# Retention attention and a low-rank mixer on one core: the first loads in another order, unscaled queries, V spread by TensorE, zero matmuls in idle time

## The chip, the core and the metric

The kernel runs on one core of a Trainium2 chip, as one launch. A core has five engines with an instruction queue each, and each works through its queue in order: TensorE (PE, matmuls into PSUM), VectorE (DVE), ScalarE (ACT), GpSimd (POOL) and SyncE (SP), which issues most of the transfers between main memory and SBUF. GpSimd issues the stores. The metric is the time of the execution on the device in microseconds, the median of several runs, lower being better. The profile is of one execution, and its span runs from the first to the last instruction.

## What is computed

```python
# q, k, v: [8, 8, 576, 64] float32 (batch, heads, positions, head dim)
scores = scale * np.matmul(q, k.transpose(0, 1, 3, 2))        # scale = 1/8
gamma = 1.0 - 2.0 ** (-5.0 - np.arange(H))
rel = pos[:, None] - pos[None, :]
Dmat = np.where(rel >= 0, gamma[:, None, None] ** rel[None, :, :], 0.0)
attn = np.matmul(scores * Dmat[None], v)
x = attn.transpose(0, 2, 1, 3).reshape(B, S, H * D)           # [8, 576, 512]
h = x.transpose(0, 2, 1) @ U @ V                              # mixes positions, rank 32
u = x + h.transpose(0, 2, 1)
out = u + np.maximum(u @ w_ch1, 0.0) @ w_ch2                  # 512 -> 2048 -> 512
```

There is no softmax: the decay is gamma to the power of the distance, so a factor per position can be put on q (gamma to the position) and its inverse on k or v, and past positions can be carried on as a 64x64 state per head.

## The kernel before

**Tiles.** Positions are cut into chunks of 128 rows. A batch has 576 = 4 x 128 + 64 rows, so two batches make nine chunks: 0 to 3 of the even batch, 5 to 8 of the odd one, and chunk 4 (`XC`), whose halves belong to one batch each. The code calls a pair of batches `p`; for the first pair the halves of chunk 4 are loaded and worked on apart (`b=0`, `b=1`; XA and XB in the load order). Four chunks in a row, of either batch, are a group of 512 rows for the two layers of the mixer: nine groups in all (`mlp`, `g`).

**One chunk.** `load` (L388) brings k, q and v and casts them to bf16; v is multiplied by `vscale` (the inverse decay, L434). For the first pair q does not come chunk by chunk: `load_q4` (L330) loads 512 rows at once, four neighbouring rows to a partition, and L347 multiplies each quarter by `qs4`, the decay of its rows. `t_q4` (L355) and `t_pe` (L476) transpose q and k on TensorE; later pairs use transposing transfers (L469). `SC` (L550) makes the scores, and L583 multiplies them by the triangle `tri`. `ST` (L510) adds k-transposed times v to the running state in `ps_s`, copied out at L543; the last copy before chunk 4 goes to `sx` (L539) by two ScalarE instructions, one for each half of the partitions. `RV` (L614) makes scores times v plus q times state, evicted to `x_t`: for later pairs at L648 on VectorE, which applies `qscale`, and for the first pair at L660 or L662 as a plain copy, mostly on ScalarE.

**The mixer.** `MA` (L677) multiplies x by U into a 32-row block per chunk, evicted to `a_sb` (L701). V (32x576) must stand four times below itself in `VV` to meet these four blocks: `load_uv` (L857) loads it, casts it (L882), copies it down three times (L874) and once more, shifted, for the odd batch (L884), all on GpSimd. `build` (L749) makes the transposed u of the first two groups directly, and `MH` (L707) the untransposed one. `mlp` (L791) runs the hidden layer `Y1` (16 units of four matmuls of 128x512), whose eviction is L813, and the second layer `Y2` (16 units of four). The weights (16 transfers of 512 KB, `load_w` L887) are cast on GpSimd (L904, L922); six staging buffers take them, four of which lie in the second `y_t`.

**Order.** Nothing is ordered by hand within an engine: `Plan` takes every operation with its engine, an estimated duration, its dependencies, a priority and the buffers that it takes and gives back, simulates the five engines and one transfer ring, and issues the instructions of each engine in the order of its planned starts. On the chip each engine keeps this order and waits by semaphores, so an operation whose data come later than planned holds up all behind it. For transfers `DMA` (L324) has two figures, the time to issue and the time in the ring. The first pair's loads are in a fixed order, the list `line` at L1022: q of batch 0, k0, V, k1 to k3, k and q of XA, v0 to v3, v of XA, U, the weights, and then q of batch 1 and the odd batch's chunks.

A variable `filler` names a bank for matmuls in idle time, but no such matmul is issued. `zer` is set to zero and not used.

Of the kernel before, what the change touches and what calls it, by code (L numbers as in the profile page):

```python
# [28 lines left out]
class Plan:  # L29
# [11 lines left out]

    def pool(self, name, n, ordered=False):
        self.pools[name] = [0.0] * n
        if ordered:
            self.line[name] = []
# [7 lines left out]
    def run(self, hint=None):  # L53
        size = {name: len(x) for name, x in self.pools.items()}
        self.pools = {name: [0.0] * n for name, n in size.items()}
        self.held = {}
# [39 lines left out]
        def earliest(o):  # L96
            t = o.ready
            for pool, key in o.acq:
                if pool in self.line and self.line[pool][0] is not o:
                    return INF  # L100
                t = max(t, min(self.pools[pool]))
            return t

        wary = bool(hint)
        while left:
# [45 lines left out]
            for pool, key in o.acq:  # L151
# [5 lines left out]
                self.held[pool, key] = i  # L157
            for x in o.rel:
                self.n_rel[x] -= 1
                self.last[x] = max(self.last.get(x, 0.0), o.vis)  # L160
                if not self.n_rel[x]:
                    self.pools[x[0]][self.held[x]] = self.last[x]
            order.append((o, e))
# [10 lines left out]
def kernel(  # L174
# [42 lines left out]
    qs4 = sbuf("qs4", [P, 2, 4, H], FP32)  # L217
# [45 lines left out]
    def consts_a():  # L263
# [15 lines left out]
        for par in range(2):  # L279
            nc.gpsimd.iota(  # L280
                qs4[:, par, :, :], pattern=[[1, 4], [0, H]], base=par * P, channel_multiplier=4,
                allow_small_or_imprecise_dtypes=True,
            )
        for h in range(H):
            nc.vector.memset(lngt[:, :, h], lng[h])
        nc.vector.tensor_tensor(
            out=qs4.rearrange("p a r h -> p (a r) h"), in0=qs4.rearrange("p a r h -> p (a r) h"),
            in1=lngt[:, 0:8, :], op=ALU.mult,
        )
        nc.scalar.activation(out=qs4, in_=qs4, func=AF.Exp, bias=0.0, scale=1.0)  # L290
# [18 lines left out]
    filler = [ps_s]  # L309
# [20 lines left out]
    def load_q4(par, prio):  # L330
# [10 lines left out]
        got = ld["q4", par] = DMA(600.0, 3300.0, fn, prio=prio, acq=keys)  # L341
        for r in range(4):
            c = 5 * par + r

            def cast(e, r=r, c=c):
                eng = nc.gpsimd if e == "POOL" else nc.vector
                eng.tensor_tensor(  # L347
                    out=qkv[slot("qkv", (0, c))][:, 0, :, :], in0=q4v(r),
                    in1=qs4[:, par, r, :, None].to_broadcast([P, H, D]), op=ALU.mult)
            st["q", c] = pl.op("DVE", 700.0, cast, [got, ld["consts"]], prio + 0.1, acq=[("qkv", (0, c))],  # L350
                               rel=[keys[r]])
            if r == 3 and par == 0:
                st["q", c].engs = [("POOL", 1300.0)]
# [34 lines left out]
    def load(p, c, prio, early=False, b=None):  # L388
# [16 lines left out]
        for n, (j, dram) in enumerate(((1, k), (0, q), (2, v))):  # L405
# [10 lines left out]
            got[j] = DMA(480.0 if len(pts) == 1 else 900.0, 1220.0 if b is None else 620.0, fn,  # L416
# [28 lines left out]
        if early:  # L445
# [9 lines left out]
            elif c == XC:  # L455
                cv.engs.append(("DVE", 700.0))
        else:
# [52 lines left out]
    def ST(p, c, prio):  # L510
# [6 lines left out]
        def fn(e):  # L517
            if first:
                filler[0] = None
# [16 lines left out]
        def ev(e):  # L536
# [8 lines left out]
            )  # L545
        st["s", c] = st["s_ev"] = pl.op("ACT", 760.0 if c == XC - 1 else 600.0, ev, [o], prio, acq=[sk],
# [3 lines left out]
    def SC(p, c, prio, with_q=True, apart=False, b=None):  # L550
# [4 lines left out]
        rk = ("ret", (p, c))  # L555
        scks = [("big", ("sc", p, c, hl)) for hl in range(2)] if apart else [("sc", (p, kb))]
# [18 lines left out]
        o = pl.op("PE", (420.0 if n == P else 250.0) + (115 if with_q else 0), fn,  # L575
# [38 lines left out]
    def RV(p, c, prio, q_done=True, b=None, in_sc=False):  # L614
# [25 lines left out]
        if has_q:  # L640
            rel.append(("sx" if c == XC else "s_sb", (p, c - 1)))
        o = pl.op("PE", 230.0 + (130 if late else 0), fn,
                  [st["ret", kb], st["v", kb], st["s", c - 1] if late else None,
# [12 lines left out]
        def part(e, hls):  # L656
            args = dict(out=xs[slot(*xk)][rows].rearrange("p hp hl d -> p hl hp d")[:, hls],
                        in_=po[rows, hls, 0:NHP * D].rearrange("p hl (hp d) -> p hl hp d", d=D))
            if e == "ACT":
                i = nc.scalar.activation(func=AF.Copy, **args)  # L660
            else:
                i = nc.vector.tensor_copy(**args)  # L662
            st.setdefault(("xi", kb), []).append(i)
            if len(st["xi", kb]) == 2:
# [411 lines left out]
```

## Time and profile before

| | |
|---|---|
| median of 6 runs | 343.15 us (338.97 to 344.69) |
| the profiled execution | 342.83 us, span 340.6 us |
| mean granted TensorE clock | 0.999 |
| last v half of batch 0 scaled (VectorE) | 19.70 to 20.52 us |
| U products evicted (`a_sb`, ScalarE) | 25.64 to 26.24 us |
| first hidden matmul (`Y1` of group 0) | 27.60 us |
| q of batch 1 there, first cast | 49.47 us |
| first hidden matmul of group 1 | 72.43 us |

Times inside the profile count from the start of the span. Instructions that follow one another are merged in a timeline: a row has the start, the length of the stretch from the first start to the last end, and the count. A matmul's recorded length contains the time in the array; matmuls in a row start closer together (64 of 128x512 in 14.2 us). "[0.64 <-DMA st_st<-in_v_dram]" means that the engine was idle for 0.64 us before it, ended by that transfer.

### The profile page before, as it was taken

To read this page: it belongs to the slowest core of one execution; us is meant where nothing else is said; L and a number is where in the kernel's file an instruction comes from. 1 tells how busy PE (TensorE), PEld (TensorE's weight loads), DVE (VectorE), ACT (ScalarE), POOL (GpSimd) and SP (SyncE) were. 2 spreads that over 40 slices of the span, in tenths; PEclk is the share of its full clock that TensorE was granted. 3 is DMA by queue.
4 is the path that set the end of the run, shared out by engine and by line. 5 is a ranking of instruction groups with operands and counts; after the bars stand their busy time and mean duration, and the time that the engine had idled before them with its cause. 6 is when DMAs were issued, how large, how long until landed. Compare 5 with 4: busy or idle time off the path is not lost.

```text
span 340.6 us, 5977 instructions
## 1 busy us (share of the span) xinstructions
PE 322.1 (95%) x2420; PEld 159.6 (47%) x2420; DVE 144.7 (42%) x230; ACT 134.4 (39%) x239; POOL 87.4 (26%) x118
## 2 busy tenths in 40 slices
PE   0799979999999999999999999999999999999994
PEld 0564435556545544544455345544544444444442
DVE  3734028776655546555466356631543010020011
ACT  3466606468601660165214621354125306404600
POOL 5957636432231312132212112310110010010010
PEclk9999999999999999999999999999999999999999
DMA  8999999998999999999999999942110240011011
GB/s 206 200 272 391 381 209 219 240 231 169 220 212 186 250 188 215 172 242 201 197 194 257 158 200 220 246 94 42 68 64 15 49 107 31 0 64 62 0 59 66
DMA packets 153386, 56.18 MB, mean 165 GB/s; under 512 B 144752, under 2 KB 146800, under 8 KB 153360
## 3 DMA queue, kind: packets, MB, share of 16 engines
q1 hardware_dynamic: 150640, 46.90, 71.3%
q0 software_dynamic: 2720, 8.92, 7.6%
q8 instruction: 19, 0.31, 0.4%
q14 instruction: 7, 0.06, 0.1%
HBM read 36.92 MB, written 9.44 MB: 136 GB/s over the span
## 4 chain that ended last, share of the span: by engine, by line
PE 83%; DMA 6%; SPq 3%; DVE 3%; POOL 1%; issue 1%; ACT 1%; DVEq 0%
PE ps_big_t L302 68%; PE ps_s L302 5%; PE ps_o L302 5%; PE ps_sc L302 4%; DMA st_st<-in_k_dram 3%; SPq L412 3%; DMA vst<-in_moe_V_dram 2%; PE ps_big_t L492 1%; DMA q_st<-in_q_dram 1%; SPq L469 1%; DVE qkv_t L347 1%; DVE ret_t L583 1%; POOL VV L874 0%; DVE o_sb L837 0%; DVE u_t L730 0%
## 5 line engine op out<-in xcount | busy, mean ns | idle before, releaser
L302 PE MATMUL ps_big_t<-uT_t,w_sb 128*128 128x512 bf16 x576 | 133.5, 379 | 0.0
L302 PE MATMUL ps_big_t<-w_sb,y_t 128*128 128x512 bf16 x576 | 133.2, 379 | 0.0
L813 ACT ACTIVATE y_t<-ps_big_t 128x512 bf16<-128x512 f32 x144 | 86.0, 597 | 94.5 <-PE ps_big_t L302 93.8
L302 PEld LDWEIGHTS <-w_sb 128*128 128x128 bf16 x576 | 53.9, 98 | 61.7 <-issue 1.4
L302 PEld LDWEIGHTS <-y_t 128*128 128x128 bf16 x576 | 53.7, 98 | 60.9 <-issue 0.5
L837 DVE TENSOR_TENSOR o_sb<-ps_big_t,u_t 128x512 f32<-128x512 f32 x36 | 24.9, 690 | 99.8 <-PE ps_big_t L302 97.2
L843 POOL DMA_DIRECT2D out_dram<-o_sb x34 | 19.4, 570 | 153.6 <-DVE o_sb L837 153.6
L434 POOL TENSOR_TENSOR qkv_t<-st_st,vscale 128x512 bf16<-128x512 f32 x34 | 35.9, 1057 | 74.0 <-DMA st_st<-in_v_dram 60.8
L583 DVE TENSOR_TENSOR ret_t<-ps_sc,tri 128x1024 bf16<-128x1024 f32 x30 | 36.6, 1221 | 22.1 <-PE ps_sc L302 22.1
L543 ACT ACTIVATE s_sb<-ps_s 128x512 bf16<-128x512 f32 x28 | 16.7, 597 | 61.6 <-PE ps_s L302 61.5
L648 DVE TENSOR_TENSOR x_t<-ps_o,qscale 128x512 bf16<-128x512 f32 x27 | 18.6, 689 | 15.9 <-PE ps_o L302 15.9
L730 DVE TENSOR_TENSOR u_t<-ps_s,x_t 128x512 bf16<-128x512 f32 x20 | 13.8, 689 | 19.0 <-PE ps_s L302 18.9
L302 PEld LDWEIGHTS <-qkT_t 64*128 64x128 bf16 (+2 forms) x576 | 15.4, 100 | 12.0 <-issue 8.9
L302 PEld LDWEIGHTS <-ret_t 128*128 128x128 bf16 (+1 forms) x320 | 13.7, 103 | 8.0 <-DVE ret_t L583 1.6
L430 DVE CAST qkv_t<-st_st 128x512 bf16<-128x512 f32 x27 | 12.0, 445 | 9.3 <-DMA st_st<-in_k_dram 9.3
L302 PE MATMUL ps_o<-qkv_t,ret_t 128*128 128x64 bf16 (+1 forms) x304 | 14.6, 196 | 0.5 <-DVE ret_t L583 0.5
L430 DVE CAST qkv_t<-q_st 128x512 bf16<-128x512 f32 x27 | 12.1, 449 | 6.5 <-DMA q_st<-in_q_dram 6.4
L501 ACT ACTIVATE qkT_t<-ps_big_t 128x512 bf16<-128x512 bf16 (+1 forms) x21 | 11.4, 558 | 6.6 <-PE ps_big_t L492 6.5
L302 PE MATMUL ps_sc<-qkT_t 64*128 64x128 bf16 (+1 forms) x296 | 13.6, 219 | 0.3 <-DVE ret_t L583 0.3
L367 PE MATMUL ps_sc<-ident,qkv_t 128*128 128x128 bf16 x32 | 3.8, 264 | 10.6 <-DVE qkv_t L347 10.5
L302 PE MATMUL ps_s<-qkv_t 128*128 128x128 bf16 (+1 forms) x128 | 13.2, 229 | 0.3 <-ACT s_sb L543 0.3
L302 PEld LDWEIGHTS <-qkv_t 128*128 128x128 bf16 (+1 forms) x128 | 9.0, 101 | 6.0 <-issue 1.7
(81 smaller groups left out, 156.5 us busy)
## 6 DMA issues: line engine op xcount, KB each, us to landing
out_dram<-o_sb POOLq DMA_DIRECT2D x34, 256.0 KB, 3.8
st_st<-in_k_dram SPq DMA_DIRECT2D x32, 256.0 KB, 5.0
st_st<-in_v_dram SPq DMA_DIRECT2D x32, 256.0 KB, 5.4
q_st<-in_q_dram SPq DMA_DIRECT2D x24, 256.0 KB, 5.0
y_t<-in_moe_w_ch_dram SPq DMA_DIRECT2D x10, 512.0 KB, 8.0
wst_t<-in_moe_w_ch_dram SPq DMA_DIRECT2D x6, 512.0 KB, 8.0
q_st<-in_q_dram SPq DMA_DIRECT2D x2, 1024.0 KB, 8.6
st_st<-in_k_dram SPq DMA_DIRECT2D x8, 128.0 KB, 5.2
```

The lines of the kernel that those rows point to most:

```text
L302: nc.tensor.matmul(*a, skip_group_check=True, **kw)
L412: sent.append(nc.sync.dma_start(out=f[rw, :, :], in_=dram[bb, :, t0:t0 + rw.stop - rw.start, :].rearrange("h s d -> s h d"),))
L430: nc.vector.tensor_copy(**args)
L434: eng.tensor_tensor(out=qkv[slot(*qk)][rows, 2, :, :], in0=at(2)[rows], in1=vscale[rows, c, :, None].to_broadcast([rows.stop - rows.start, ...
L501: nc.scalar.activation(func=AF.Copy, **args)
L543: nc.scalar.activation(out=s_sb[slot(*sk)], in_=ps_s.rearrange("p (a b) -> p a b", b=P), func=AF.Copy)
L583: nc.vector.tensor_tensor(out=ret[slot(*rk)][rows, hl, :, 0:n], in0=bank(hl.start)[rows, None, :, 0:n] if apart else ps_sc[rows, hl, :, 0: ...
L648: nc.vector.tensor_tensor(out=xs[slot(*xk)][rows].rearrange("p hp hl d -> p hl hp d"), in0=po[rows, :, 0:NHP * D].rearrange("p hl (hp d) - ...
L730: nc.vector.tensor_tensor(out=us[slot(*uk)].rearrange("p (hp hl d) -> p hp hl d", hl=2, d=D), in0=bank().rearrange("p (hp hl d) -> p hp hl ...
L813: nc.scalar.activation(out=y1s[slot(*yk)][:, f, :], in_=ps_big[slot(*bk)], func=AF.Relu)
L837: nc.vector.tensor_tensor(out=osb[slot(*ok)], in0=ps_big[slot(*bk)], in1=us[slot(*uk)], op=ALU.add)
L843: eng.dma_start(out=out_flat[row:row + P, :], in_=osb[slot(*ok)])
```

## The change

- The fixed load order of the first pair is new. V moves behind U; the chunks of k and v take turns.
- q of the first pair is cast without a factor, on VectorE or ScalarE; the factor is put on at the x eviction, which so becomes the VectorE product for all whole chunks. `qs4` goes away. The halves of chunk 4 keep their scaled q and have a plain copy on ScalarE.
- V is cast by ScalarE and spread to 128 partitions by a matmul with `rep4`, four identities side by side, in two pieces by way of `ps_s`.
- The copy to `sx` before chunk 4, in the first pair, is one half on ScalarE and one on VectorE.
- Banks: the scores of chunk 4 go to `ps_sc`, and the product of chunk 1 to `ps_o`.
- The planner asks for as many free buffers as an operation takes of a pool; some estimates change; it keeps when buffers are held. Before the first `Y1`, where it sees TensorE idle for long enough and finds a bank free, zero matmuls of 128x512 are issued, up to 14 in one gap.

```diff
+    def idle(self, banks, a, b):
+        for x in banks:
+            if all(end < a or begin > b for begin, end in self.spans.get(x, [])):
+                return x
+        return None
...
-                t = max(t, min(self.pools[pool]))
+                n = sum(x[0] == pool for x in o.acq)
+                t = max(t, sorted(self.pools[pool])[n - 1])
...
-        for par in range(2):
-            nc.gpsimd.iota(
-                qs4[:, par, :, :], pattern=[[1, 4], [0, H]], base=par * P, channel_multiplier=4,
-                allow_small_or_imprecise_dtypes=True,
-            )
...
-        nc.scalar.activation(out=qs4, in_=qs4, func=AF.Exp, bias=0.0, scale=1.0)
+        for i in range(4):
+            nc.vector.tensor_copy(out=rep4[:, i * R:(i + 1) * R], in_=ident[0:R, 0:R])
...
-        got = ld["q4", par] = DMA(600.0, 3300.0, fn, prio=prio, acq=keys)
+        got = ld["q4", par] = DMA(600.0, 3900.0 - 600.0 * par, fn, prio=prio, acq=keys)
...
-                eng = nc.gpsimd if e == "POOL" else nc.vector
-                eng.tensor_tensor(
-                    out=qkv[slot("qkv", (0, c))][:, 0, :, :], in0=q4v(r),
-                    in1=qs4[:, par, r, :, None].to_broadcast([P, H, D]), op=ALU.mult)
-            st["q", c] = pl.op("DVE", 700.0, cast, [got, ld["consts"]], prio + 0.1, acq=[("qkv", (0, c))],
-                               rel=[keys[r]])
-            if r == 3 and par == 0:
-                st["q", c].engs = [("POOL", 1300.0)]
+                args = dict(out=qkv[slot("qkv", (0, c))][:, 0, :, :], in_=q4v(r))
+                if e == "ACT":
+                    nc.scalar.activation(func=AF.Copy, **args)
+                else:
+                    nc.vector.tensor_copy(**args)
+            st["q", c] = pl.op("DVE", 390.0, cast, [got], prio + 0.1, acq=[("qkv", (0, c))], rel=[keys[r]],
+                               alt=[("ACT", 640.0)])
...
-            got[j] = DMA(480.0 if len(pts) == 1 else 900.0, 1220.0 if b is None else 620.0, fn,
+            got[j] = DMA(480.0 if len(pts) == 1 else 900.0, 1220.0 if b is None else 900.0, fn,
...
+            elif c in (2, 3):
+                cv.engs.append(("DVE", 800.0))
...
+        if p == 0 and c == XC - 1:
+            insts = []
...
+            h = [pl.op(e, 390.0, lambda e, w=w: half(e, w), [o], prio, acq=[sk] if e == "ACT" else [],
+                       rel=[st["pss"]]) for e, w in (("ACT", slice(0, HALF)), ("DVE", slice(HALF, P)))]
...
-        if p:
+        def ev_x(e):
+            nc.scalar.activation(out=xs[slot(*xk)][rows].rearrange("p hp hl d -> p hl hp d"),
+                                 in_=po[rows, :, 0:NHP * D].rearrange("p hl (hp d) -> p hl hp d", d=D),
+                                 func=AF.Copy)
+        if b is None:
             st["x", kb] = [pl.op("DVE", 700.0, ev, [o], prio, rel=[pk])]
-        elif b == 0 or c == NCH - 1:
-            st["x", kb] = [pl.op(e, 400.0, lambda e, i=i: part(e, slice(i, i + 1)), [o], prio, rel=[pk])
-                           for i, e in enumerate(("ACT", "DVE"))]
         else:
-            st["x", kb] = [pl.op("ACT", 610.0, lambda e: part(e, slice(0, 2)), [o], prio, rel=[pk])]
+            st["x", kb] = [pl.op("ACT", 610.0, ev_x, [o], prio, rel=[pk])]
...
-        cv = pl.op("POOL", 600.0, lambda e: gp.tensor_copy(out=VV[0:R, 0:S], in_=vst), [ld["lv"]], -970.0)
-        ld["V"] = pl.op("POOL", 1500.0, rep, [cv], -970.0)
+        cv = pl.op("ACT", 640.0, lambda e: nc.scalar.activation(out=VV[0:R, 0:S], in_=vst, func=AF.Copy),
+                   [ld["lv"]], -935.0)
+        got = None
+        for i, (n, w) in enumerate((("V", slice(0, 4 * P)), ("Vx", slice(4 * P, S)))):
+            bk = ("pss", n)
+            m = w.stop - w.start
...
+                mm(ps_s[:, 0:m], rep4, VV[0:R, w], start=True, stop=True)
...
+                nc.scalar.activation(out=VV[:, w], in_=ps_s[:, 0:m], func=AF.Copy)
+            r = pl.op("PE", 230.0, fr, [cv, ld["consts"], got], -934.0 + 700.0 * i, acq=[bk])
+            got = ld[n] = pl.op("ACT", 600.0 - 300.0 * i, er, [r], -934.0 + 700.0 * i, rel=[bk])
...
-            SC(0, c, pr + 3, with_q=False, apart=c in (0, 2, XC), b=b)
+            SC(0, c, pr + 3, with_q=False, apart=c in (0, 2), b=b)
...
-            RV(0, c, pr + 1, q_done=False, b=0 if c == XC else None, in_sc=c in (1, 3))
+            RV(0, c, pr + 1, q_done=False, b=0 if c == XC else None, in_sc=c == 3)
...
-    line = [ld["q4", 0], ld["k", (0, 0)], ld["lv"]] + [ld["k", (0, c)] for c in range(1, 4)]
-    line += [ld["k", (0, XA)], ld["q", (0, XA)]]
-    line += [ld["v", (0, c)] for c in range(4)] + [ld["v", (0, XA)], ld["lu"]] + ld["lw"]
-    line += [ld["q4", 1]] + [ld[x, (0, XB)] for x in "kqv"]
-    line += [ld["k", (0, c)] for c in range(5, NCH)] + [ld["lub"]]
-    line += [ld["v", (0, c)] for c in range(5, NCH)]
+    line = [ld["q4", 0]] + L("k0 k1 v0 k2 v1 k3 v2 kA qA v3 vA") + [ld["lu"], ld["lv"]] + ld["lw"]
+    line += [ld["q4", 1]] + L("k5 kB k6 qB v5 vB k7 v6 k8") + [ld["lub"]] + L("v7 v8")
...
+    until = min(o.start for o in pl.ops if o.name == "Y1")
+    homes = {("big", i): ps_big[i] for i in range(3)}
+    homes["pss", 0] = ps_s
     with tc.manual_schedule():
+        at = 1000.0
         for o, e in order:
+            if e == "PE":
+                a, b = at + 60.0, o.start - 120.0
+                n = int((b - a) / 220.0)
+                if o.start <= until and n > 0:
+                    x = pl.idle(homes, a, b)
+                    if x is not None:
+                        for _ in range(min(n, 14)):
+                            mm(homes[x], zer[:, 0:P], zer, start=True, stop=True)
+                at = o.end
             o.fn(e)
```

## The prediction

> **What bounds the kernel now.** I read the page first (busy shares, the slices, the chain that ended last), then TensorE's waits, then busy time by stretch, then the timelines of TensorE, VectorE and GpSimd up to 75 us.
>
> ```profile
> PE 322.1 (95%) x2420; PEld 159.6 (47%) x2420; DVE 144.7 (42%) x230; ACT 134.4 (39%) x239; POOL 87.4 (26%) x118
> ...
> PEclk9999999999999999999999999999999999999999
> DMA  8999999998999999999999999942110240011011
> ...
> PE 83%; DMA 6%; SPq 3%; DVE 3%; POOL 1%; issue 1%; ACT 1%; DVEq 0%
> ```
>
> TensorE is busy 95% of the span and is 83% of the chain. The DMA row is full up to slice 26 (about 222 us), so an earlier TensorE can run into a late transfer. The waits of TensorE name where it stands still:
>
> ```profile
> PE ps_sc L367 <- DVE qkv_t L347: 10.5, 4, 7.3
> PE ps_big_t L302 <- ACT a_sb L701: 0.7, 1, 0.7
> ```
>
> Of the 10.5 us, 7.3 are the start and 2.1 lie at 48 to 50 us. By stretch (columns: TensorE, weight loads, VectorE, ScalarE, GpSimd, clock, DMA share, GB/s):
>
> ```profile
> 27.60:41.80 14.20, 14.20 (x67) 6.46 (x66) 3.11 (x6) 9.32 (x16) 9.93 (x10) 1.00 1.05 388
> 41.80:48.10 6.30, 6.28 (x30) 2.65 (x27) 0.69 (x1) 0.61 (x2) 3.83 (x4) 1.00 1.09 227
> 48.10:50.20 2.10, 0.00 (x0) 0.00 (x0) 0.73 (x2) 0.00 (x0) 0.01 (x1) 1.00 0.89 245
> 50.20:72.40 22.20, 21.75 (x256) 12.45 (x257) 16.62 (x24) 13.07 (x26) 10.90 (x13) 1.00 0.97 226
> ```
>
> The first hidden matmul starts at 27.60. From there to TensorE's last matmul at 336.4 there are 308.8 us, 305.1 of them busy in the same view: only 3.7 us of waiting is left. So the change can win in two places: an earlier 27.60, and less of those 3.7 us (2.13 at 48.1, 0.26 at 52.6, 0.49 at 150, 0.59 at 195). The lines of the timelines:
>
> ```profile
> 17.43 0.64 PE L302 MATMUL ps_o<-qkv_t,ret_t 128*128 128x64 bf16 x8
> ...
> 21.52 0.61 PE L302 MATMUL ps_big_t<-x_t,UU 128*32 128x512 bf16 x1
> 22.06 0.52 PE L302 MATMUL ps_s<-qkv_t 128*128 128x128 bf16 x4
> 22.42 0.40 PE L302 MATMUL ps_sc<-qkv_t,ret_t 128*128 128x64 bf16 x8
> ...
> 27.60 3.65 PE L302 MATMUL ps_big_t<-uT_t,w_sb 128*128 128x512 bf16 x16
> ```
>
> ```profile
> 19.70 0.82 DVE L434 TENSOR_TENSOR qkv_t<-st_st,vscale 64x512 bf16<-64x512 f32 x1 [0.64 <-DMA st_st<-in_v_dram]
> ...
> 66.71 0.98 DVE L430 CAST qkv_t<-q_st 128x512 bf16<-128x512 f32 x1
> ```
>
> ```profile
> 20.95 0.32 POOL L878 CAST UU<-ust 128x160 bf16<-128x160 f32 x1 [0.97 <-DMA ust<-in_moe_U_dram]
> 22.08 1.04 POOL L904 CAST w_sb<-wst_t 128x1024 bf16<-128x1024 f32 x1 [0.81 <-DMA wst_t<-in_moe_w_ch_dram]
> 23.38 1.04 POOL L904 CAST w_sb<-wst_t 128x1024 bf16<-128x1024 f32 x1 [0.26 <-DMA wst_t<-in_moe_w_ch_dram]
> ```
>
> The same eight 128x64 matmuls take 0.64 at 17.43 and 0.40 at 22.42: TensorE is slow until about 22 us, though the PEclk row shows nothing of it. The last half chunk of v is there at 19.67, yet the hidden matmuls start 8 us later: TensorE is busy for 3.60 of the 3.60 us from 22.0 to 25.6 with what piled up, because all of v came after all of k. First-layer weights are cast at 24.42, which is a floor for 27.60.
>
> **The change, part by part.** *Load order.* The same bytes move ahead of the last v chunk, less the 72 KB of V (0.35 at the 205 GB/s of the first stretch), so it lands at 19.35 instead of 19.67 and U at 20.6. SyncE issues as many transfers as before; V's is moved past the k, v and U transfers and now lands behind U, at about 20.95 (0.35 after it). But v0 to v2 land between their k's at about 10.3, 12.9 and 15.6 (1.3 us per chunk after q4 at 6.5 and k0 at 7.75). Three of four state matmuls and evictions leave the 17 to 21 us stretch.
>
> *Late path.* Last v 19.35, scaled by 20.2 (0.82), its products by 21.1 (0.43 and 0.44), ScalarE's eviction by 21.75 (0.60), the last U matmul by 22.15 (0.38), and the a_sb eviction can start then. On the same ScalarE now stand V's cast (nearest row: 0.63 for 128x512), and the copy of its spread (0.60); between them a matmul (0.38). With V in at 20.95 they end at 22.7. If ScalarE's order has x first, V's cast pushes a_sb to 22.5, and the copy of the spread (0.60) ends after it: with the 1.96 us that before has from the start of a_sb (25.64) to 27.60, the hidden matmuls start at 22.5 + 1.96 + 0.6 = 25.05. If V is first, x waits for 22.7, a_sb starts at 23.8 and the hidden matmuls at 25.75. I take 25.4: **2.2 us earlier**. Queued behind V's cast on ScalarE are x and a_sb; behind the spread matmul on TensorE stand the last v products. The whole wait is in these two ends. The floor of 24.42 is not reached.
>
> *GpSimd* loses V's cast (0.81), three copies (2.42) and one q scaling (1.54), all before 12 us. Its v scalings follow their loads; V's second copy (0.66) moves behind the weight casts, which arrive at a DMA's pace (0.3 us idle ahead of each). Worth nothing beyond earlier v.
>
> *q casts.* Three products of 1.07 each on VectorE become casts of 0.43; in batch 1 four, 3.35 us in all, become 1.7. On the path it counts where q4 is waited for: 0.69 to 0.43 for the first in batch 1, and 0.3 taken. The constants lose two iotas, a product and an exponential (0.30, 0.23, 0.26) and gain four 32x32 copies, with no row: a 128x32 memset took 0.09, a 64x64 copy 0.23, so 0.4 to 0.9, I take 0.4. All hidden: VectorE waits 3.71 us for q4 there. Without that cover it would cost that 0.4.
>
> *Weighed, the port.* The row: a q cast beside a GpSimd product (66.37 to 67.41) took 0.98, elsewhere 0.42. The Trainium skill, "SBUF — State Buffer", section "Who interferes with whom", goes further: VectorE's cast in a two-port mode and any GpSimd instruction exclude each other wholly, so a cast could stand 1.04 before it runs its 0.43. That speaks against casts in the place of products. By the row four casts cost up to 3.9 us in batch 1, by the rule up to 5.9. But GpSimd idles until 50.91 there and until v0 in batch 0, so at most two meet it: 0.5 by the row, 2.1 by the rule. I go by the row.
>
> *x evictions* of eight chunks go from ScalarE (0.60) to VectorE (0.69, since q is unscaled). In batch 0 VectorE idles 3.9 us ahead of 24.4; they fit. In batch 1 VectorE gets 4 x 0.69, less 0.41 for the half that it had, less 1.6 of casts: 0.7 more on 17.35 busy of the 23.0 us from 49.4 to 72.4. The split sx copy is 0.4 instead of 0.78: counted in the path. The scores' banks move (two chunks to the single ps_sc or ps_o): each waits for a 1.2 mask or a 0.7 eviction, with chunks 2.6 us apart; nothing.
>
> *Zero matmuls.* Bounds of one: 0.22 (spacing of the first layer, 14.2 us over 64) to 0.43 slow, at most 14 in a gap: 6.0 us, which fits from the memset's end at 1.13 to the first transpose at 7. Later they stand in planned gaps: TensorE idled 2.9 us from 7 to 20, so if none of the gaps is real, 2.9 lost; if they make 16 to 22 us run as after 22, up to 2 gained. *Weighed, the clock.* The granted row is full throughout while the durations halve at 22. "TensorE: Matmul & The Clock Gate", Part 1, has the array at half rate until a window of about 3.4 us was busy: an estimate from it is full rate by 8 us, 2 us gained in 16 to 22. By the waits seen, transfers pace that stretch after reordering, and I count nothing beyond the path above, which already uses fast durations. It also says that an idle window slows it again; 2.13 us idle at 48 did not (0.40 for a transposition of four after it).
>
> *The wait at 48.* q4 of batch 1 lands at 49.44 behind the weights; those bytes are the same, so it stays. TensorE has done 7 of 16 second-layer units (0.86 each) when it comes to that wait. The planner now dates that load 1.44 later (0.6 for the first q4, 3 x 0.28 for half chunks) and its cast 0.31 shorter: 1.3 units more ahead; an earlier start of 2.2 gives 2.5 more. 3.8 units are 3.3 us: TensorE arrives at 48.1 - 2.2 + 3.3 = 49.2 and goes on at 49.9. So 0.7 is left of 2.39: **1.7 gained**. Ends: 2.4 gained, or, with no unit moved, 1.9 lost.
>
> *Batch 1 and after.* With 3.3 us less filler VectorE has 18.1 us of work in about 19.7. I take a new wait of **0.7** (0 to 2.5). Loads are issued behind transposes that wait for computing (the chain at 140 to 149 and 183 to 194), so they move with TensorE; **0.2** for the new order.
>
> **Sum.** 2.2 + 1.7 - 0.7 - 0.2 = 3.0. The profiled execution took 342.83 (span 340.6), 0.32 below the median of six, 343.15: I forecast 340.1 for the median, 339.8 for a run like the profiled one.
>
> **Rivals.** *The transfer keeps its time*: no second-layer unit moves ahead, TensorE stands until 49.9 and only the cast, the 0.26 and little else is won: 342.5. For it: DMA full, q4's landing fixed. Against: the planner's dates do move. *All of it comes*: matmuls from 24.5 and both waits at 48 and 52 gone: 3.1 + 2.4 + 0.3 = 5.8, 337.3. For: the weights allow it. Against: V lands last and has three steps. *VectorE becomes the bound in batch 1*: it is in order, so a cast that waits for a load or for GpSimd holds masks and x's behind it. If its 18.1 us stretch to more than 24 (0.98 per cast, masks waiting), TensorE waits 4 us there and the gain is gone; at 27 it is 346.7. For: 92% load; against: the port is mostly free then. *It isn't filled*: zero matmuls that stand ahead of ready work are in the range of the first.
>
> **Chances.** Main case 0.50 (338.7 to 341.5), the transfer 0.20, all of it 0.17, VectorE 0.13. The kernel's measurement tells about 1% (3.4 us) from no change: faster means under 339.7. Two fifths of the main case and all of the third: 0.37. Slower by over 1%: two thirds of the last, 0.09. Within: 0.54. The range 337.2 to 343.5 leaves out half of the third case and most of the last.
>
> **What would show it.** First hidden matmul at 25.4 (25.0 to 25.8); slow matmuls gone by 8 us; TensorE's idle before batch 1's q4 transposes under 1 us with 10 or 11 units ahead; VectorE's casts 0.43; the first hidden matmul of the second group near 69.5 (72.43 before). Wrong if the first stays above 27, if the idle at 48 grows to 4, or if masks wait behind casts after 50.

## The result and the profile after

| | before | changed |
|---|---|---|
| median | 340.93 us (66 runs, 338.51 to 345.29) | 341.75 us (29 runs, 340.65 to 343.74) |
| the profiled execution, span | 342.83, 340.6 | 341.92, 340.1 |
| mean granted TensorE clock | 0.999 | 0.985 |
| first hidden matmul of group 0 | 27.60 | 29.65 |
| transposes of batch 1's q begin on TensorE | 50.21 | 50.86 |
| first hidden matmul of group 1 | 72.43 | 73.12 |
| last matmul of TensorE ends | 336.35 | 336.12 |

The ratio of the two is 1.0035, with the interval 1.002 to 1.005: no gain, where 340.1 and a gain of 3.0 were forecast. The ratios and intervals, here and below, are taken over the runs that lie within 1.5% of their kernel's fastest, which leaves out 14 of the 66 of before and none of the 29 of the changed kernel (and 8 of 21 in the ninth experiment); the means of all runs, 341.54 and 341.96, are too near to each other, for the spread of before, to tell a small cost from none. The six runs of before that the forecast started from had a median of 343.15, and were high by 2.2 us.

Some of the time lies outside the span: 2.1 to 2.3 us in the runs of before, 1.72 to 1.85 in those of the changed kernel. So 0.4 of the 0.91 us by which the two profiled executions differ was won there. No term of the forecast held it, and what it is was not looked into.

The page of the changed kernel, its busy shares, two rows of slices (one slice is 8.5 us) and the chain:

```profile
PE 329.7 (97%) x2447; PEld 160.9 (47%) x2447; DVE 146.3 (43%) x236; ACT 135.1 (40%) x239; POOL 79.3 (23%) x108
...
PEclk9967999999999999999999999999999999999999
DMA  8989999999999999999999999922110230011012
...
PE 87%; SPq 4%; DVE 3%; DMA 3%; issue 1%; POOL 0%; DVEq 0%
```

TensorE's busy time is up by 7.6 us. The zero matmuls are one part of it; the clock row shows another: slices 2 and 3, counted from 0 (17 to 34 us), have 0.6 and 0.7, and the row had no such place before. The stretches of 2 us show its shape (columns: TensorE busy and its instructions, granted clock, DMA share, GB/s):

```profile
12.00:14.00 2.00, 1.78 (x29) 1.00 1.36 218
14.00:16.00 2.00, 1.22 (x24) 1.00 1.42 165
16.00:18.00 2.00, 1.18 (x27) 1.00 1.09 155
18.00:20.00 2.00, 0.88 (x16) 0.88 0.39 99
20.00:22.00 2.00, 1.86 (x23) 0.50 0.97 302
...
26.00:28.00 2.00, 2.00 (x8) 0.50 1.06 409
28.00:30.00 2.00, 2.00 (x7) 0.56 1.07 389
```

For six microseconds, from 14 to 20, the array is busy for 3.28 us, 55% of the time and falling, and the clock is halved for about 10 us, from 19.5 to 29.8. That is the stretch in which the path to the first hidden matmul lies. TensorE's timeline, from the zero matmuls at the start to that matmul, and two rows of ScalarE and VectorE:

```profile
1.19 5.49 PE L303 MATMUL ps_big_t<-zer 128*128 128x512 bf16 x14 [1.19 <-DVE zer L273]
...
15.30 0.40 PE L303 MATMUL ps_sc<-qkT_t 64*128 64x128 bf16 x8 [0.69 <-ACT qkT_t L502]
...
16.33 0.38 PE L303 MATMUL ps_s<-qkv_t 128*128 128x128 bf16 x4 [0.42 <-POOL qkv_t L433]
...
18.00 0.29 PE L493 MATMUL ps_big_t<-ident,qkv_t 64*128 64x64 bf16 x4 [0.49 <-POOL qkv_t L439]
...
19.94 0.59 PE L303 MATMUL ps_s<-qkv_t 128*128 128x128 bf16 x4 [0.87 <-POOL qkv_t L433]
...
25.14 1.03 PE L303 MATMUL ps_sc<-ident,x_t 128*128 128x128 bf16 x8
26.10 0.23 PE L303 MATMUL ps_s<-VV,rep 32*128 32x64 bf16 x1
26.27 1.03 PE L303 MATMUL ps_big_t<-VV,a_sb 128*128 128x512 bf16 x2
...
28.80 1.06 PE L303 MATMUL ps_big_t<-zer 128*128 128x512 bf16 x2
29.65 1.09 PE L303 MATMUL ps_big_t<-uT_t,w_sb 128*128 128x512 bf16 x4
```

```profile
28.19 0.60 ACT L783 ACTIVATE uT_t<-ps_sc 128x512 bf16<-128x512 f32 x1 [0.68 <-PE ps_sc L303]
28.19 0.69 DVE L785 CAST uT_t<-ps_sc 128x512 bf16<-128x512 f32 x1 [0.16 <-PE ps_sc L303]
```

Four state matmuls take 0.38 at 16.33 and 0.59 at 19.94. The waits in brackets go with taking k and v in turns: GpSimd scales a chunk's v (L433), or the q of XA (L439), as it comes, or ScalarE evicts its transposes (L502), and TensorE, which before worked through a heap, now follows them. No single wait reaches 0.9 us.

One more thing stands in these rows. The last two pieces of the transposed u, on which the first hidden matmuls work, are evicted by 28.79 and 28.88, and TensorE is through with its own work at 28.80. Then come two zero matmuls, and only behind them, 0.85 us later, the first hidden matmul. The planner saw idle time there, and on the chip there was hardly any.

The wait at 48 to 50 us has gone, but look at the starts (before: L367 at 50.21, after 2.13 of waiting):

```profile
39.64 4.48 PE L303 MATMUL ps_big_t<-uT_t,w_sb 128*128 128x512 bf16 x20
43.96 7.07 PE L303 MATMUL ps_big_t<-w_sb,y_t 128*128 128x512 bf16 x32
50.86 1.06 PE L366 MATMUL ps_sc<-ident,qkv_t 128*128 128x128 bf16 x16
```

The load of q landed at 47.23; TensorE, late by then, came to it at 50.86. It has eight second-layer units (32 matmuls) ahead of the transposes, one more than before. The sum closes: the first hidden matmul is 2.05 later, the waits after it went from 3.66 to 1.61, the work between is 0.2 shorter, and the last matmul ends 0.23 earlier. What the changed kernel still waits for after 29.65:

```profile
PE ps_o L303 <- DVE ret_t L599: 0.7, 1, 0.7
PE ps_sc L303 <- DVE ret_t L599: 0.3, 1, 0.3
PE ps_s L303 <- DVE x_t L665: 0.2, 1, 0.2
```

### The profile page after: what moved, and what is told of

It reads as the page before. It is cut to its first block, busy times and chain, and to the rows that moved or that the text cites. A ratio compares the mean times of both kernels' runs of the same rounds, so it can differ in the third digit from the quotient of the medians.

```text
span 340.1 us, 6027 instructions
## 1 busy us (share of the span) xinstructions
PE 329.7 (97%) x2447; PEld 160.9 (47%) x2447; DVE 146.3 (43%) x236; ACT 135.1 (40%) x239; POOL 79.3 (23%) x108
## 4 chain that ended last, share of the span: by engine, by line
PE 87%; SPq 4%; DVE 3%; DMA 3%; issue 1%; POOL 0%; DVEq 0%
PE ps_big_t L303 73%; PE ps_o L303 5%; PE ps_s L303 5%; SPq L411 4%; PE ps_sc L303 4%; DMA st_st<-in_v_dram 2%; DVE ret_t L599 1%; DMA st_st<-in_k_dram 1%; DVE x_t L665 1%; PE ps_big_t L493 1%; DVE qkv_t L429 0%; DVE o_sb L840 0%; PE ps_sc L366 0%; POOL qkv_t L433 0%; POOL UU L878 0%
## 5 line engine op out<-in xcount | busy, mean ns | idle before, releaser
L433 POOL TENSOR_TENSOR qkv_t<-st_st,vscale 128x512 bf16<-128x512 f32 x34 | 35.7, 1050 | 80.7 <-DMA st_st<-in_v_dram 63.6
L599 DVE TENSOR_TENSOR ret_t<-ps_sc,tri 128x1024 bf16<-128x1024 f32 x30 | 36.6, 1221 | 22.5 <-PE ps_sc L303 22.5
L665 DVE TENSOR_TENSOR x_t<-ps_o,qscale 128x512 bf16<-128x512 f32 x34 | 23.4, 688 | 14.1 <-PE ps_o L303 13.9
L733 DVE TENSOR_TENSOR u_t<-ps_s,x_t 128x512 bf16<-128x512 f32 x20 | 13.8, 689 | 19.5 <-PE ps_s L303 19.4
L429 DVE CAST qkv_t<-st_st 128x512 bf16<-128x512 f32 x27 | 13.5, 500 | 10.5 <-DMA st_st<-in_k_dram 10.3
L502 ACT ACTIVATE qkT_t<-ps_big_t 128x512 bf16<-128x512 bf16 (+1 forms) x22 | 11.9, 561 | 9.4 <-PE ps_big_t L493 9.3
L733 DVE TENSOR_TENSOR u_t<-ps_o,x_t 128x512 bf16<-128x512 f32 x16 | 10.9, 684 | 1.2 <-PE ps_o L303 1.2
```

The source lines that it names most:

```text
L433: eng.tensor_tensor(out=qkv[slot(*qk)][rows, 2, :, :], in0=at(2)[rows], in1=vscale[rows, c, :, None].to_broadcast([rows.stop - rows.start, ...
L599: nc.vector.tensor_tensor(out=ret[slot(*rk)][rows, hl, :, 0:n], in0=bank(hl.start)[rows, None, :, 0:n] if apart else ps_sc[rows, hl, :, 0: ...
L665: nc.vector.tensor_tensor(out=xs[slot(*xk)][rows].rearrange("p hp hl d -> p hl hp d"), in0=po[rows, :, 0:NHP * D].rearrange("p hl (hp d) - ...
L733: nc.vector.tensor_tensor(out=us[slot(*uk)].rearrange("p (hp hl d) -> p hp hl d", hl=2, d=D), in0=bank().rearrange("p (hp hl d) -> p hp hl ...
```

## The experiments

Twelve experiments ran; the fourth is the kernel before without an edit, the eleventh repeats the sixth. The letters in the expectations are names for theories, in the order in which they came up. Of those that come to matter, A says that the slow stretch of TensorE is what the change lost its time by, D that the order of the loads brings that stretch on, K that unscaled queries cost VectorE time in batch 1. "Before" with another median is the same kernel before, run again on the chip of that experiment.

**1. Keep the array busy.** The planner issues zero matmuls only where it finds a bank free for the whole gap; from 12.8 to 28.8 us it finds none. This version writes them into the bank that the next matmul overwrites anyway (`own_bank`, left out below, looks it up), and adds three that add zero to the state.

```diff
...
-                    if x is not None:
+                    bank = homes[x] if x is not None else own_bank(o)
+                    if bank is not None:
                         for _ in range(min(n, 14)):
-                            mm(homes[x], zer[:, 0:P], zer, start=True, stop=True)
+                            mm(bank, zer[:, 0:P], zer, start=True, stop=True)
+                if o is sts[0]["ST", XC - 1]:
+                    for _ in range(3):
+                        mm(ps_s, zer[:, 0:P], zer, start=False, stop=True)
```

> The changed kernel, with zero matmuls also where no bank stands idle: then they go into the bank that the next real matmul overwrites, and three that add zero to the state go ahead of the fourth state matmul, so that TensorE has work in its gaps from 14 to 20 us. Theory A (TensorE falls back to half rate at about 20 us because its gaps from 14 to 20 stay empty, and works off 9 us of dense work slowly): no slow stretch, first hidden matmul at 25 to 26 instead of 29.65, then about 1 us of waiting for batch 1's q, 2 to 3.5 us less than the changed kernel in all, ratio to the kernel before 0.990 to 0.996. Rival B (the late path of v, V and ScalarE sets the first hidden matmul, the rate doesn't matter): it stays at 28.5 or later and the time within 0.7 us of the changed kernel.

341.69 us (20 runs) against 341.08 of before (55): 1.0028 (1.0007 to 1.0049). The clock is 1.00 throughout, and the stretches read:

```profile
14.00:16.00 2.00, 1.96 (x33) 1.00 1.40 165
16.00:18.00 2.00, 1.56 (x30) 1.00 1.18 158
18.00:20.00 2.00, 1.89 (x20) 1.00 0.52 110
20.00:22.00 2.00, 1.63 (x31) 1.00 0.99 311
```

Its timeline has the first hidden matmul at 26.18, 3.47 earlier than the changed kernel's, and eight transposes in 0.62 that took 1.03:

```profile
23.69 0.62 PE L303 MATMUL ps_sc<-ident,x_t 128*128 128x128 bf16 x8
24.24 0.20 PE L303 MATMUL ps_s<-VV,rep 32*128 32x64 bf16 x1
24.44 0.60 PE L303 MATMUL ps_big_t<-VV,a_sb 128*128 128x512 bf16 x2
...
25.75 0.59 PE L303 MATMUL ps_big_t<-zer 128*128 128x512 bf16 x2
26.18 3.62 PE L303 MATMUL ps_big_t<-uT_t,w_sb 128*128 128x512 bf16 x16
...
49.08 1.14 PE L366 MATMUL ps_sc<-ident,qkv_t 128*128 128x128 bf16 x16 [0.97 <-ACT qkv_t L348]
...
81.49 0.41 PE L303 MATMUL ps_o<-qkv_t,ret_t 128*128 128x64 bf16 x8 [0.45 <-DVE ret_t L599]
...
149.01 0.41 PE L303 MATMUL ps_o<-qkv_t,ret_t 128*128 128x64 bf16 x8 [0.83 <-DVE ret_t L599]
```

So the fall-back and its size at the first hidden matmul are shown, and yet the median does not move (341.69 and 341.75), where A expected 2 to 3.5 us less. Where the 3.47 went can be read at the milestones: 1.78 is left at the transposes of batch 1's q, 1.70 at the first hidden matmul of group 1 (71.42), 0.58 at the last matmul (335.54). TensorE now waits for q's load (landed 48.37), and later for masks. What holds a mask at 149 is on VectorE:

```profile
147.39 0.43 DVE L429 CAST qkv_t<-st_st 128x512 bf16<-128x512 f32 x1 [1.86 <-DMA st_st<-in_k_dram]
147.73 1.22 DVE L599 TENSOR_TENSOR ret_t<-ps_sc,tri 128x1024 bf16<-128x1024 f32 x1
```

The mask (L599) stands behind the cast of a k chunk that waits 1.86 us for its load. The changed kernel has this wait too (0.73 at 150), but not the one at 81. Transfers come in their own time here, and an earlier TensorE runs into them.

**2. The changed kernel without zero matmuls** (the condition for issuing them made false).

> The changed kernel without any zero matmul. Theory A: the array is slow from the start, as in the kernel before, and turns fast once the dense stretch is under way, at 21 to 25 us, and stays so; first hidden matmul at 27 to 28.5, 1 to 2.5 us less than the changed kernel. Rival B (zero matmuls do no harm, the order of work does): first hidden matmul at 29.5 or later, time as the changed kernel or above.

341.72 (20 runs), 1.002 (1.0001 to 1.0039). The clock falls here too, from 20.9 to 27.7 us; the first hidden matmul is at 28.13. The zero matmuls do not start the slow stretch. They change how often it comes: the mean clock was under 0.992 in 9 of these 20 runs, in all 29 of the changed kernel, and in none of the 55 of before. The 9 runs took 341.5 on average and the other 11 took 341.9, so in this plan the slow stretch, as far as the clock row shows it, has no price in the time.

Two more readings. The array was fast without any zero matmul long before the 21 to 25 us that A expected: eight matmuls of 64x128, which take 0.61 at the slow rate, took 0.47 at 10.43 and 0.40 from 11.47 on. And the first hidden matmul comes 1.52 before that of the changed kernel, though the clock is halved on its path here too: the fall comes 1.4 us later, and no zero matmuls stand ahead of it.

**3. Before with zero matmuls**, by the changed kernel's rule (the same loop and the record of held buffers that it needs).

> The kernel before with nothing but the zero matmuls put in by the changed kernel's rule. Theory A: it begins fast; whether it stays so depends on the gaps that are left, which are fewer from 12 to 25 us than in the changed kernel (0.5 and 0.34 us long), so it stays fast, the first hidden matmul comes at 26 to 27 instead of 27.60, but batch 1's q still lands at 49.4, so the time falls by less than 0.5 us. Rival C (zero matmuls make any kernel here fall back at about 20 us): a slow stretch appears and it is 1 to 3 us slower than the kernel before.

342.17 (20 runs), 1.0003 (0.9976 to 1.0029). They bring the array up early, and then it has something to lose. In the profiled execution, one of 7 in 20 whose mean clock was under 0.992, the fall at 23.0 comes 1.8 us after the end of one long hole (a wait of 1.56 us for the cast of U, which is loaded behind all of v):

```profile
18.00:20.00 2.00, 1.62 (x40) 1.00 0.95 256
20.00:22.00 2.00, 0.81 (x13) 1.00 0.87 250
22.00:24.00 2.00, 2.00 (x35) 0.76 0.86 235
24.00:26.00 2.00, 2.00 (x12) 0.50 1.03 379
```

Its first hidden matmul was at 30.32, with five zero matmuls in the 4.2 us ahead of it.

**4. Before again**, unedited, for a second profile.

> The kernel before, unchanged, for a second trace of it: its times lie from 338.5 to 345.3. Theory A: the moment at which its array turns fast differs from execution to execution (22 us in the first trace), and the time follows it. Otherwise: the moment is the same within 0.5 us.

One run of 339.85. The first hidden matmul was at 27.02 and the last matmul ended at 333.35, 3.0 before the first profile's. Its timeline at the wait:

```profile
41.30 6.21 PE L302 MATMUL ps_big_t<-w_sb,y_t 128*128 128x512 bf16 x28
48.06 0.40 PE L367 MATMUL ps_sc<-ident,qkv_t 128*128 128x128 bf16 x4 [0.55 <-DVE qkv_t L347]
```

0.55 us of waiting, not 2.13: q landed at 47.28 here, at 49.44 there. So 1.6 us of the wait that the forecast counted on belong to one execution. Which of the two is nearer to the usual is not known: the first took 1.9 us more than the median of 340.93, this one 1.1 less. The moment at which the array turns fast moves as well: 21.0 here, 22 there.

From its first hidden matmul to its last this execution took 306.33 us, and the changed kernel 306.47 (the first profile of before 308.75). Beside this one, the changed kernel's lateness at the first hidden matmul, 2.63, is nearly the whole of its lateness at the last, 2.77.

**5. The changed kernel with the old order of loads.**

```diff
-    line = [ld["q4", 0]] + L("k0 k1 v0 k2 v1 k3 v2 kA qA v3 vA") + [ld["lu"], ld["lv"]] + ld["lw"]
+    line = [ld["q4", 0]] + L("k0") + [ld["lv"]] + L("k1 k2 k3 kA qA v0 v1 v2 v3 vA") + [ld["lu"]] + ld["lw"]
```

> The changed kernel with the first loads of batch 0 in the order of the kernel before (all of k, then all of v, V second); the odd batch's loads, the zero matmuls and all else as changed. Theory D (k and v in turns leave TensorE with too little work from 14 to 20 us, and that lets the rate fall; all of v after all of k makes one dense stretch): no slow stretch between 20 and 28 us, first hidden matmul at 25.5 to 27.5. Rival E (the rate falls because zero matmuls stop at 13 us, whatever the order): it is slow from about 20 us here too and the first hidden matmul comes at 28.5 or later. In both the time is within 1 us of the changed kernel, since batch 1's q lands at 47 to 49.5 in all traces.

341.49 (20 runs) against 341.7 (47), 1.0012 (0.9982 to 1.0041). The clock stays at 1.00 under the same rule for zero matmuls: TensorE is busy 1.08 of 2 us in 14 to 16, but 1.59 in 16 to 18, 1.87 in 18 to 20, and all of 20 to 22. First hidden matmul 26.30, almost that of the first experiment. This speaks for D: what loading in turns spreads out, loading k before v heaps up where the array needs it. It is not the order alone, though: with other planned gaps three zero matmuls fall into the stretch (two at 15.65, one at 18.49), where the changed kernel has none between 12.8 and 28.8. Of the time it says little, like the first.

**6. The first experiment with a later date for batch 1's q.** Since that load became the next limit, its estimated time in the ring is raised by 1.7 us for the second batch (3300 to 5000), so that the planner puts more second-layer units ahead of it. No operation is added or left out.

```diff
-        got = ld["q4", par] = DMA(600.0, 3900.0 - 600.0 * par, fn, prio=prio, acq=keys)
+        got = ld["q4", par] = DMA(600.0, 3900.0 + 1100.0 * par, fn, prio=prio, acq=keys)
```

> The kernel kept busy from 14 to 20 us, and the planner told that batch 1's q needs 1.8 us longer in the ring, so that it puts about two more second-layer units ahead of the wait for it. Theory F (the 3.5 us won at the first hidden matmul in that kernel were lost to planned order: TensorE stands at loads that land later than planned): the 0.97 us wait at 49 is gone, no new wait as long in batch 1, 0.5 to 1.2 us less than without, ratio to the kernel before 0.997 to 1.000. Rival G (transfers and VectorE pace batch 1, whatever is put ahead): the wait comes back between 55 and 72 us, and the time stays at 341.4 to 342.

339.32 (12 runs), 0.9964 (0.9938 to 0.9989). First hidden matmul 26.22. This is faster than before, and within 0.8 us of the forecast.

**7. Before with only the loads in turns** (`line`: k and v alternating from chunk 1 on; the scores of chunk 4 in `ps_sc`, which that order needs).

> The kernel before with k and v of batch 0 loaded in turns (q, k0, V, k1, v0, k2, v1, k3, v2, k and q of XA, v3, v of XA), and the scores of chunk 4 in ps_sc as in the changed kernel; no zero matmuls, q scaled, V copied by GpSimd. Theory D: less work piles up, so the array turns fast late or turns fast and falls back; slow matmuls between 20 and 25 us, first hidden matmul at 27.5 to 29.5, 0 to 1.5 us slower than the kernel before. Rival H (the order is good by itself, the harm is in the other parts): first hidden matmul at 26.5 or earlier and 0.5 us or more faster.

343.49 (4 runs), 1.0108 (1.0032 to 1.0183). Without zero matmuls early on, and with TensorE following the loads, eight 128x64 matmuls still take 0.61 at 19.00 and at 24.98: the array never leaves its slow rate before the first hidden matmul, which comes at 32.47.

**8. The sixth experiment with the old order of loads** (the edits of 5 and 6 together).

> The first loads in the order of before, zero matmuls also into the next matmul's own bank, and batch 1's q planned 1.8 us later, the rest as changed. Theory D with F: fast throughout, first hidden matmul at 25 to 26.5, no wait above 0.5 us for batch 1's q, ratio to the kernel before 0.992 to 0.998. Rival G: waits of 2 us or more between 40 and 72 us and a ratio of 1.000 to 1.004.

341.86 (20 runs), 1.0023 (0.9998 to 1.0048), first hidden matmul 26.82, clock full. The reverse of what the fifth suggests: with the array kept fast and q dated late, the kernel with the new order is 2.5 us faster in median. Its timeline has no wait at q (ten units, then the transposes at 49.70). Of the 2.5 us, 0.6 is there at the first hidden matmul of the profiled executions, and 0.3 lies outside the span (2.12 against 1.78 us); where the rest goes was not found, for its profiled execution took 340.84, among the fastest of its runs.

**9 and 10. The later date alone,** in before (estimate 3300 + 1800 for batch 1) and in the changed kernel (the line of the sixth).

> The kernel before with nothing changed but the planner's date for batch 1's q, 1.8 us later. Theory F (the loss after an early first hidden matmul is planned order, and the date is the lever): about two more second-layer units ahead of that q, no wait there, 0.5 to 1.5 us faster than the kernel before (ratio 0.996 to 0.9985). Rival G (the transfers pace the stage, and what TensorE does ahead is only moved): the first hidden matmul of the second group stays 22.5 to 23.5 us behind the landing of that q and the ratio lies within 0.999 to 1.001.

> The changed kernel with that date 1.8 us later and its slow stretch from 20 to 29 us left in. TensorE is so late there that it does not wait for the q at all. Theory F: nothing to win, within 0.5 us of the changed kernel (ratio to before 1.001 to 1.005), so that the slow stretch costs its price as soon as the order is right. Rival J (the date alone explains the 339.3 of the kernel with both): 339 to 340.2.

In before: 343.06 (21 runs, 339.26 to 348.66) against 341.68 (73), ratio 1.0017 (0.9987 to 1.0046): no gain. In the changed kernel: 341.56 (21 runs), 1.0008 (0.9988 to 1.0027). Its timeline shows why the date does nothing for a late TensorE:

```profile
44.32 8.80 PE L303 MATMUL ps_big_t<-w_sb,y_t 128*128 128x512 bf16 x39
52.95 1.06 PE L366 MATMUL ps_sc<-ident,qkv_t 128*128 128x128 bf16 x16
```

Two more units, so the transposes come 2.1 us later than in the changed kernel, though q was there at 47.48. The clock had the slow stretch in all 21 runs.

**11. The sixth again,** on another chip with more runs.

> The kernel with work for TensorE from 14 to 20 us and the later date for batch 1's q, once more, for a closer ratio and a second trace. Theory F: 0.9945 to 0.9985 of the kernel before, first hidden matmul at 26.2, no wait for the q. If it was the luck of twelve runs: 1.000 to 1.003.

339.62 (21 runs, 338.26 to 340.9) against 341.68 (73): 0.9955 (0.9935 to 0.9974). It is the best version of all: first hidden matmul 26.13, first of group 1 at 70.43, last matmul's end 333.82. Its timelines of TensorE and of VectorE:

```profile
43.03 6.76 PE L303 MATMUL ps_big_t<-w_sb,y_t 128*128 128x512 bf16 x29 [0.34 <-POOL w_sb L934]
49.63 1.06 PE L366 MATMUL ps_sc<-ident,qkv_t 128*128 128x128 bf16 x16
```

```profile
145.60 1.23 DVE L599 TENSOR_TENSOR ret_t<-ps_sc,tri 128x1024 bf16<-128x1024 f32 x1 [0.73 <-PE ps_sc L303]
146.86 0.43 DVE L429 CAST qkv_t<-st_st 128x512 bf16<-128x512 f32 x1
```

No wait at q. And a second effect that the date was not meant to have: the plan as a whole came out in another order, and here the mask stands before the cast of k. TensorE's 0.83 at 149 is gone, as is the 0.45 at 81. How the 2.07 us between the first and this experiment divide into the two was not tried apart.

**12. The eleventh with batch 1's q scaled as before** (VectorE product, plain copies of x by ScalarE for chunks 5 to 8).

> That kernel with batch 1's q multiplied by its decay again (on VectorE, 0.69 us each, before the masks) and the x evictions of chunks 5 to 8 plain copies on ScalarE again. Theory K (VectorE paces batch 1 from 60 to 67 us, where its masks and x evictions follow one another without a pause): 2.8 us of evictions leave VectorE there, the first hidden matmul of the second group comes 0.5 to 1.5 us earlier against the landing of batch 1's q, and the time falls by 0.3 to 1 us. Rival G (the last v loads pace it): no change, within 0.4 us.

340.88 (21 runs), 1.0003 (0.9986 to 1.0021), 1.3 us slower than the eleventh. In 49.6 to 70.4 VectorE is busy for 13.46 instead of 15.38 us, as K would have it, and group 1 starts 0.24 earlier (70.19); but waits of 0.72 at 149 and 0.54 at 152 are back. Of the 1.3 us, 0.4 lies outside the span (2.14 against 1.77 us), and the profiled execution took 342.85, the slowest of the 21, so the two waits may be larger in it than usual. K is not borne out: the time does not fall when VectorE has less to do in batch 1. The test is not clean, because the plan came out in another order from the start (first hidden matmul 26.73, 0.6 later).

## Why the prediction was wrong

**First hidden matmul at 25.4, 2.2 us gained: wrong, and the largest term.** It came at 29.65. The steps up to the array's work hold: the last v half landed at 19.23 (19.35 predicted), and was scaled from 19.25 to 20.43; V was cast from 20.90 to 21.57 and two q casts took 0.76. What failed is the sentence that the path "already uses fast durations", and beside it the dismissal of the fall-back. The forecast itself quoted the Trainium skill, "TensorE: Matmul & The Clock Gate", Part 1, that an idle window slows the array again, and set against it that 2.13 us of idling at 48 had not. That row answered another question: one hole between dense stretches. Here the array idled for 45% of six microseconds, in pauses under 0.9 us each, and it fell. The same page's section "A second HAM failure mode: psum-queue depth-cycling" is nearer to this: it tells of another kernel, in which frequent short pauses between groups of matmuls made the rate go down and up again. Here it went down once. What decides it is not settled by these traces; the share of busy time alone does not. In the six microseconds up to the fall TensorE was busy for 62% (changed), 57% (second experiment) and 66% (third), and around the wait at 48, where the rate held, for 65% (46 to 52).

The forecast also saw that loading in turns takes work out of the 17 to 21 us stretch, and took this for a pure gain. The zero matmuls of the start did what it hoped: slow matmuls were gone by 7 us, and came back at 19.5.

With the array fast the step is off by 0.8 (26.18 against 25.4), and its working can be followed: V's cast went first on ScalarE, which was the later of the two ends; x was evicted from 22.62 (22.7 in the working), `a_sb` from 23.79 (23.8). From there to the first hidden matmul it was 2.39 us instead of 1.96. The 0.43 between them is the two zero matmuls at 25.75: without them the chain would have ended at 25.75, which is the end that the working gives for V first. The forecast named zero matmuls ahead of ready work as a danger and counted nothing for them.

So the 4.25 us between 25.4 and 29.65 divide into 3.47 that go when the array is kept fast (among them 0.42, since the same two zero matmuls took 0.85 at the slow rate), 0.43 for these two matmuls at the fast rate, and 0.35 because V came first. The first part was measured; the second is read from the rows, and these two matmuls alone were not taken out.

**The wait at 48, 1.7 gained: its size was one execution's.** It is 2.13 us in one profile of before and 0.55 in the other, and the landing that was taken as fixed at 49.44 came at 47.28, 47.23 and 48.37 in other executions. And 3.8 units were to move ahead, 3.3 us of work; one did (eight, after seven). In the changed kernel the wait vanished because TensorE was late. With an early TensorE (first experiment) 0.97 of it was still there, and it went only when the raised date put two more units ahead.

**New waits in batch 1, 0.7: right as a number.** From 50.86 to 73.12 TensorE waited 0.32, 0.10 and 0.23 us for x and masks. There is luck in it, for the reason given, 3.3 us less second-layer work there, did not come about: one unit of 0.86 went ahead. The rival that made VectorE the bound is out in the changed kernel: it had TensorE wait 4 us, and VectorE was busy for 16.9 of the 22.3. In the paragraph on the port, two casts at 0.98 instead of 0.43 would make 1.1, not 0.5; none of batch 1's q casts was that slow here, VectorE's two took 0.42 each.

**0.2 for the new order: too small once TensorE is early.** The first experiment loses 1.3 us to masks behind late k casts at 81 and 149, of which the changed kernel had 0.7 already, at 150. It is the mechanism that the VectorE rival described, at other places than it named.

**The rival that a transfer keeps its time** comes nearest (342.5), but not by its mechanism: in the changed kernel TensorE does not stand at q at all. Its mechanism shows in the first experiment, where the 3.47 us of an earlier start shrink to 1.78 at q's landing.

**The baseline.** The 0.32 between the profiled run and the median of six was accounted for, but that median was taken as given, and it stood 2.2 high. Against 340.93 the whole forecast is a gain of 0.8 us, and the version that makes its two conditions true (array kept fast, q dated late) measures 339.6. Neither does it alone: 341.69 with the array kept fast, 341.56 with the late date. The late date also put masks and casts in another order, so its two effects are not told apart.

What stays open: why the eighth experiment gains nothing, though both conditions hold in it; and why the runs of before spread over 6.8 us (standard deviation 1.8) and those of the changed kernel over 3.1 (0.8).

## What to carry to other kernels

Spreading work out to follow its loads is not free on TensorE: before counting a path with fast durations, add up how busy the array stays in the few microseconds ahead of it, and compare the clock row with the durations. Filler that a plan puts into idle time can stand ahead of ready work on the chip; look at what it delays. A wait seen in one profile is worth what it is over several executions; take a second profile before counting on its removal. Where a planner orders everything, an estimate that is only a number can be worth more than the operations that are saved, and an earlier engine needs its neighbours' dates moved too.

## What the runs showed of the hardware

- The clock row starts at 1.00 while the array is slow: in before it reads 1.00 from the start, with durations that halve at 22 us. It showed the slow rate only after a fall from the fast one. Durations are the safer reading.
- Matmuls with zero operands raise the rate: after fourteen of them from 1.19 us on, four transposes took 0.40 at 8.18 us, where before the rate was reached at 22. They are not the only way: without them, in the second experiment, the rate was there at about 10.5.
- The array can fall back to half the rate without a long pause: in the changed kernel no wait from 14 us on reached 0.9 us, and the clock was 0.50 from 19.5 to 29.8.
- The instruction queue's packets of 16 KB share the DMA engines with the data. The page of before counts them in one line:

```profile
q8 instruction: 19, 0.31, 0.4%
```

The weights land every 1.35 us (512 KB each). In the first profile of before a gap of 2.58 us (to 36.39) has such a packet at 34.0, which took 1.10 us on one of the 16 DMA engines; in the first experiment a gap of 2.75 us (26.95 to 29.70) has one of 1.06 at 27.4. But a gap of 2.40 us (to 25.73) has none in it, and in the second profile of before packets at 18.6 and 33.2 went with gaps of 1.48 and 1.57 only. Whether they cause the late landings, and with them the spread of before, was not tried.
